# Attention and a gated FFN on one core: batch 1's rounds later in block 0, batch 2's q and k loaded earlier

## The chip, the cores and the metric

The kernel runs on one core of a Trainium2 chip. The metric is the device time of one execution in microseconds. The engines are PE (TensorE, matrix multiply; PEld is its weight load), DVE (VectorE), ACT (ScalarE), POOL (GpSimd) and SP (SyncE, which here only issues DMAs). POOL and ACT issue some DMAs too.

## The reference

```python
# q, k, v: 8 batches, 8 heads, 576 positions, 64 dims, float32
scores = q @ k^T / sqrt(64)            # per batch and head
scores = where(pos_i // 64 >= pos_j // 64, scores, -1e9)
attn = softmax(scores)
x = (attn @ v)                          # heads side by side: [8 * 576, 512]
out = (relu(x @ w_gate) * (x @ w_val)) @ w_out   # 512 -> 1536 -> 512
```

The mask works in blocks of 64 positions: a query sees all keys of its own block and of earlier ones. Inputs and output are float32; the kernel computes in bfloat16 and accumulates in float32.

## The kernel before

**Work units.** A batch has 512 main positions and a tail of 64 (512 to 575). A *round* r handles head pair hp = r % 4 of batch b = r // 4 for the main positions: `visit(r)` computes the transposed scores of both heads on PE, three groups of exp on ACT write `attnT`, `corners(r)` lets DVE clear the masked corners, `head_av(r, hh)` multiplies with v for one head (10 matmuls) and normalises on DVE into `xnat`, and `pe_xT(r)` (four PE transposes and an ACT copy) or `to_xT_dma(r)` (a DMA transpose on SP) puts the result into `xT`, the transposed input of the FFN. `tail_visit`, `tail_av` and `tail_to_xT` do the same for a batch's 64 tail positions, all heads at once.

**The FFN as the clock of the program.** `ffn_gen` (L602) is a generator that yields after each of its matmuls. Block j is the FFN of batch j's main positions: 96 matmuls for gate and value (12 column groups f, for each 4 parts c of gate and 4 of value, where c is the head pair), then 48 for the output (4 row groups s of 12). Block 8 is the FFN of all tails. A *place* p is a count of these matmuls: block j runs from place 144 j to 144 (j + 1). Attention is placed between the matmuls: `run(base, events)` (L758) sorts events by place, issues FFN matmuls up to each place and then calls the event. The rounds of batch b are placed inside block b - 1, so `xT` of batch b must be whole when place 144 b is reached. Only in block 0, f = 0, are the matmuls ordered so that the two of c = 3 come last (L611).

**Order.** All five engines run in the order in which the program is written (`manual_schedule`, L669): an instruction that waits holds up all later ones of its engine. A DMA that waits holds up its issuing engine.

**Loads.** For batches 0 to 3, class `Early` loads float32 into `stage` buffers (ten of them) with DMAs from SP, and an engine casts to bfloat16: `load_qk(h0, n)` and `cast_qk` for n heads from h0 (cast order q, then k), `load_v_packed` and `cast_v_packed` for v of four heads with four positions side by side, which `sort_v` (16 PE matmuls with the selection matrix `sel`, then a DVE and an ACT copy) has to put in order, `load_v` and `cast_v` for v already in order with one DMA for each head, `load_v_chunks` the same for 256 positions of all heads, `load_tails` and `cast_tails`, `cast_v_tail` for the 64 tail positions. q and k are then transposed, by `pe_mains(hp)` on PE (four transposes for q, evacuated by DVE, four for k, evacuated by ACT) or by `transpose` (DMA into `perm`) and `unpermute` (`un`; DVE for q, POOL for k). From batch 4 on, `load_qkv` (L304) loads with casting DMAs from POOL, and `dma_transposes` transposes with DMAs from SP.

**Buffers that matter here.** `psum_ffn` has three banks, shared by gate, value, output, AV and transposes; `ob`, the copy of an output row group that is stored, has three buffers; `q_bf` and `k_bf` have two each; `v_bf`, `qTm`, `kTm`, `qTt`, `kTt` have one for even and one for odd batches. A row group's store is issued when the next row group's copy has been (L645 to L647): that of s = 0 in block 0 at place 120. `put` (L591) issues the stores of batch 0 from POOL, later ones from ACT.

**Block 0 before.** After the first 32 matmuls of the FFN (from L728), the loads of w_out, batch 1's second halves and the tails of batches 0 and 1 are written, then the casts for POOL, in this order: batch 1's q and k of heads 0 to 3, w_gate and w_val's last part, packed v, w_out, batch 1's second q, k and v, all tails. Batch 1's `pe_mains(0)`, `pe_mains(1)` and `sort_v(0)` stand at places 64, 68 and 72, the rounds 4 to 7 at 76, 88, 100 and 118. Batch 2's loads are written at 111 (`load_2`) and its casts at 124 (`mains_2`).

Of the kernel before, what the change touches and what calls it, by code (L numbers as in the profile page):

```python
# [17 lines left out]
def kernel(  # L18
# [10 lines left out]
    nc = tc.nc  # L29
# [89 lines left out]
    class Early:  # L119
# [59 lines left out]
        def cast_qk(self, h0, n, engs):  # L179
            lo = 64 * (h0 % 4)  # L180
            for t in range(2):
                engs[t](  # L182
                    self.half(t, h0 // 4)[:, :, lo : lo + 64 * n].rearrange(
                        "p j (h d) -> p h j d", d=64
                    ),
                    self.st[t, h0].rearrange("p (h j d) -> p h j d", h=n, j=4),
                )
# [414 lines left out]
    def ffn_gen():  # L602
        for j in range(B + 1):
            hT = []
            x = xT_of(j) if j < B else xTt.rearrange("p b h n -> p h b n")
            for f in range(12):
                i, fo = f // 4, 128 * (f % 4)
                gate = psum_ffn.tile([128, 512], FP, name="ffnp")
                val = psum_ffn.tile([128, 512], FP, name="ffnp")
                steps = [(t, c) for t in range(2) for c in range(4)]  # L610
                if j == 0 and f == 0:  # L611

                    steps.sort(key=lambda tc_: tc_[1] == 3)
# [55 lines left out]
    with tc.manual_schedule(engines={E.PE, E.DVE, E.Activation, E.Pool, E.SP}):  # L669
# [60 lines left out]
        e1.load_qk(4, 4)  # L730
        e1.load_v_packed(4)
        for e in (e0, e1):
            e.load_tails((0, 1))
            e.load_tails((2,))
        e1.cast_qk(0, 4, (pool, pool))
        cast_w(w_2, pool)
# [3 lines left out]
        cast_w(w_out[2], pool)  # L740
        e1.cast_qk(4, 4, (pool, pool))
        e1.cast_v_packed(4, pool)
        for e in (e0, e1):
            e.cast_tails((pool, pool))
            e.cast_v_tail(pool)
        ffn(32)
        e1.pe_mains(0, (dve, act))
        ffn(4)
        e1.pe_mains(1, (dve, act))
        ffn(4)  # L750
        e1.sort_v(0, (dve, act))
        ffn(4)
        place = [76]

# [4 lines left out]
        def run(base, events):  # L759
            for p, f in sorted(events, key=lambda e: e[0]):  # L760
                upto(base + p)
                f()

        def round_at(p, r, av, to_xT, late=(), corner_eng=None):

            exps = []

            def begin():
                exps.extend(visit(r))
                exps[0]()  # L770
                exps[1]()

            return [
                (p, begin),
                (p + 6, lambda: exps[2]()),
                (p + 13, lambda: corners(r, corner_eng or nc.vector)),
                (av[0], lambda: head_av(r, 0)),
                (av[1], lambda: head_av(r, 1)),
                (to_xT[0], lambda: to_xT[1](r)),
            ]  # L780
# [23 lines left out]

        early = {}

        def load_2():
            e2 = early[2] = Early(2)
            e2.load_qk(0, 4)
            e2.load_qk(4, 4)  # L810
            e2.load_v_chunks(0)
            e2.load_v_chunks(1)
            e2.load_tails((0, 1))
            e2.load_tails((2,))

        def mains_2():
            e2 = early[2]
            e2.cast_qk(0, 4, (pool, pool))
            e2.cast_qk(4, 4, (pool, pool))
            e2.transpose(0)  # L820
            e2.transpose(1)

        def tails_2():
            e2 = early[2]
            e2.cast_tails((pool, pool))
            e2.transpose_tails()

        def v_2():
            e2 = early[2]
            e2.cast_v_tail(pool)  # L830
            e2.cast_v_chunks(0, pool)
            e2.cast_v_chunks(1, pool)
# [23 lines left out]

        events = []
        for r, p in ((4, 76), (5, 88), (6, 100), (7, 118)):
            end = 20 if r == 6 else 14
            events += round_at(p, r, (p + end + 2, p + end + 6), (p + end + 10, pe_xT))  # L860
        events += [
            (98, lambda: e1.pe_mains(2, (dve, act))),
            (110, lambda: e1.pe_mains(3, (dve, act))),
            (111, load_2),
            (116, lambda: e1.sort_v(4, (dve, act))),
            (124, mains_2),
            (140, lambda: e0.pe_tails((dve, act))),
        ]
        run(0, events)
        events = tail_at(4, 0, (20, 24)) + tail_at(116, 1, (132, 136))  # L870
        for r, p in ((8, 32), (9, 52), (10, 72), (11, 92)):
            events += round_at(p, r, (p + 21, p + 25), (p + 25, to_xT_dma))
        events += [
            (7, lambda: e1.pe_tails((dve, act))),
            (8, tails_2),
# [16 lines left out]
        for b in range(3, B):  # L892
            events = tail_at(120, b, (136, 140))
            if b == 3:
                events += tail_at(50, 2, (69, 73))
            for i, p in enumerate((2, 26, 74, 96) if b == 3 else (2, 32, 62, 92)):
                r = 4 * b + i
                events += round_at(p, r, (p + 20, p + 24), (p + 24, to_xT_dma))
            if b == 3:
                events.append((3, un(3, 2, (dve, pool))))  # L900
                events.append((33, un(3, 3, (dve, pool))))
            if b + 1 < B:
                for at, which in ((4, (0, 1)), (75 if b == 3 else 46, (2,))):
                    events.append((at, lambda b=b, w=which: load_qkv(b + 1, w)))
                events.append((66, lambda b=b: dma_transposes(b + 1)))
            run(144 * (b - 1), events)
# [30 lines left out]
```

## Time and profile before

| | us |
|---|---|
| median of 8 executions | 373.5 (372.23 to 376.93) |
| the profiled execution | 376.93 |
| its span | 375.1 |
| PE busy | 356.6 |
| DVE, ACT, POOL busy | 170.4, 171.3, 119.2 |
| block 0's first matmul (PE) | 20.27 |
| block 1's first matmul | 66.74 |

The profile is one execution, taken by the hardware profiler. A row of a group or of the order of time gives the line of the kernel, the engine, the operation, what is written and read, and how often (x); in the order of time it begins with start and duration in us, and what stands in brackets is the idle time of the engine before it and what ended that. A row of waits names who waited, for whom, the total in us, how many times and the longest. A row of a stretch gives its length and then each engine's busy time. POOL's casts of 128x1024 take 1.04 us each, those of 64x512 0.61; a matmul of 512 columns is issued every 0.216 us at full clock. A DMA row ends with the time from issue to landing.

### The profile page before, as it was taken

To read this page: it belongs to the slowest core of one execution; us is meant where nothing else is said; L and a number is where in the kernel's file an instruction comes from. 1 tells how busy PE (TensorE), PEld (TensorE's weight loads), DVE (VectorE), ACT (ScalarE), POOL (GpSimd) and SP (SyncE) were. 2 spreads that over 40 slices of the span, in tenths; PEclk is the share of its full clock that TensorE was granted. 3 is DMA by queue.
4 is the path that set the end of the run, shared out by engine and by line. 5 is a ranking of instruction groups with operands and counts; after the bars stand their busy time and mean duration, and the time that the engine had idled before them with its cause. 6 is when DMAs were issued, how large, how long until landed. Compare 5 with 4: busy or idle time off the path is not lost.

```text
span 375.1 us, 7513 instructions
## 1 busy us (share of the span) xinstructions
PE 356.6 (95%) x2956; PEld 178.1 (47%) x3004; DVE 170.4 (45%) x392; ACT 171.3 (46%) x283; POOL 119.2 (32%) x156
## 2 busy tenths in 40 slices
PE   7899969999999999699999999999999999999995
PEld 3644434544555545244554445444544454444443
DVE  3644455556555444155334542554345444323432
ACT  5924744576435652355445534653366423302310
POOL 6678776455267174480058003000000000000000
PEclk9999999999999999899999999999999999999999
DMA  8999999979959699999779965845200130020013
GB/s 256 295 371 358 373 202 302 188 177 264 140 130 134 88 130 154 139 125 148 135 95 132 125 128 93 65 78 133 79 16 17 42 100 7 2 84 28 3 34 106
DMA packets 140739, 51.35 MB, mean 137 GB/s; under 512 B 120352, under 2 KB 133920, under 8 KB 140704
## 3 DMA queue, kind: packets, MB, share of 16 engines
q0 software_dynamic: 56576, 8.13, 44.8%
q1 hardware_dynamic: 79424, 34.62, 42.4%
q10 hardware_dynamic: 4704, 8.13, 7.1%
q8 instruction: 23, 0.38, 0.4%
q14 instruction: 12, 0.10, 0.2%
HBM read 37.75 MB, written 9.44 MB: 126 GB/s over the span
## 4 chain that ended last, share of the span: by engine, by line
PE 82%; DMA 10%; POOL 2%; issue 2%; DVE 1%; ACT 1%; SPq 1%; POOLq 0%; DVEq 0%; ACTq 0%
PE ffnp L615 45%; PE ffnp L634 23%; PE ffnp L553 5%; DMA stage<-in_moe_w_val_dram 3%; DMA stage<-in_k_dram 3%; PE sc L426 3%; DMA xT<-xnat 3%; PE ffnp L522 2%; PE one L426 1%; DMA stage<-in_q_dram 1%; PE sc L460 1%; POOL k_bf L182 1%; SPq L132 1%; POOL sel L94 0%; POOL q_bf L182 0%
## 5 line engine op out<-in xcount | busy, mean ns | idle before, releaser
L628 DVE TENSOR_TENSOR hT<-gate_sb,ffnp 128x512 bf16<-128x512 bf16 x108 | 74.2, 687 | 99.6 <-PE ffnp L615 84.3
L624 ACT ACTIVATE gate_sb<-ffnp 128x512 bf16<-128x512 f32 x108 | 65.0, 602 | 105.6 <-PE ffnp L615 105.4
L615 PE MATMUL ffnp<-xT,wg 128*128 128x512 bf16 x369 | 100.7, 382 | 3.9 <-DMA xT<-xnat 3.2
L615 PE MATMUL ffnp<-xT,wv 128*128 128x512 bf16 x376 | 101.6, 382 | 0.7 <-ACT gate_sb L624 0.2
L634 PE MATMUL ffnp<-wo,hT 128*128 128x512 bf16 (+1 forms) x420 | 98.1, 373 | 1.1
L615 PEld LDWEIGHTS <-wv 128*128 128x128 bf16 x432 | 40.3, 98 | 50.2 <-issue 7.3
L615 PEld LDWEIGHTS <-wg 128*128 128x128 bf16 x432 | 40.2, 98 | 47.1 <-issue 4.3
L634 PEld LDWEIGHTS <-hT 128*128 128x128 bf16 x444 | 40.2, 98 | 40.0 <-issue 0.8
L435 ACT ACTIVATE attnT<-sc 128x1024 bf16<-128x1024 f32 x56 | 56.9, 1040 | 0.0
L644 DVE COPY ob<-ffnp 128x512 f32<-128x512 f32 (+1 forms) x37 | 25.1, 677 | 40.8 <-PE ffnp L634 40.4
L316 POOL DMA_DIRECT2D v_bf<-in_v_dram x20 | 16.8, 856 | 64.3 <-PE ffnp L522 48.6
L553 PEld LDWEIGHTS <-attnT 128*128 128x128 bf16 x640 | 26.4, 98 | 15.2 <-DVE xnat L508 4.4
L507 DVE RECIPROCAL recip<-ffnp 128x4 f32<-128x4 f32 (+1 forms) x76 | 13.6, 179 | 37.0 <-PE ffnp L553 26.8
L553 PE MATMUL ffnp<-v_bf,attnT 128*128 128x65 bf16 x600 | 28.2, 194 | 0.4 <-PE sc L460 0.2
L441 ACT ACTIVATE attnT<-one 128x256 bf16<-128x256 f32 x28 | 10.7, 383 | 35.1 <-PE ffnp L426 26.9
L508 DVE TENSOR_TENSOR xnat<-ffnp,recip 128x256 bf16<-128x256 f32 x60 | 25.5, 424 | 2.1
L426 PE MATMUL sc<-qTm,kTm 64*128 64x512 bf16 (+1 forms) x168 | 16.8, 305 | 0.0
L426 PEld LDWEIGHTS <-kTm 64*128 64x128 bf16 x224 | 8.8, 94 | 14.9 <-issue 10.6
L481 ACT ACTIVATE attnTt<-one 64x256 bf16<-64x256 f32 x8 | 3.0, 376 | 28.0 <-PE ffnp L460 28.0
L472 ACT ACTIVATE attnTt<-sc 128x1024 bf16<-128x1024 f32 x16 | 15.6, 1014 | 0.0
L316 POOL DMA_DIRECT2D k_bf<-in_k_dram x16 | 14.1, 897 | 3.9 <-DMA v_bf<-in_v_dram 3.6
L316 POOL DMA_DIRECT2D q_bf<-in_q_dram x16 | 14.3, 918 | 0.1
(88 smaller groups left out, 262.7 us busy)
## 6 DMA issues: line engine op xcount, KB each, us to landing
out_dram<-ob ACTq DMA_DIRECT2D x28, 256.0 KB, 2.3
stage<-in_moe_w_gate_dram SPq DMA_DIRECT2D x6, 512.0 KB, 9.1
stage<-in_moe_w_val_dram SPq DMA_DIRECT2D x6, 512.0 KB, 9.5
stage<-in_q_dram SPq DMA_DIRECT2D x6, 512.0 KB, 6.4
stage<-in_k_dram SPq DMA_DIRECT2D x6, 512.0 KB, 7.3
stage<-in_moe_w_out_dram SPq DMA_DIRECT2D x6, 512.0 KB, 9.6
stage<-in_v_dram SPq DMA_DIRECT2D x8, 256.0 KB, 6.9
q_bf<-in_q_dram POOLq DMA_DIRECT2D x16, 128.0 KB, 6.5
```

The costliest lines, as they stand in the source:

```text
L316: nc.gpsimd.dma_start(dst, src[b, :, 128 * c : 128 * c + n, :].rearrange("h p d -> p h d"),)
L426: nc.tensor.matmul(where[c].rearrange("p (c n) -> p c n", n=128), kTm[b % 2][head_of(hh), c, hp, :], qTm[b % 2][head_of(hh), c:4, hp, :], ...
L435: return lambda: nc.scalar.activation(at[:, :, lo : lo + 512], sc, AF.Exp, scale=scale)
L472: return lambda: nc.scalar.activation(at[:, :, 2 * i : 2 * i + 2, 0:256], main[i].rearrange("p g (h n) -> p g h n", h=2), AF.Exp, scale=scale,
L507: nc.vector.reciprocal(recip, av[:, :, 64])
L508: nc.vector.tensor_tensor(out=out, in0=av[:, :, 0:64], in1=recip.to_broadcast([rows, n, 64]), op=AX.mult,)
L553: nc.tensor.matmul(av[:, p, :], at[:, hh, col : col + 128], vb[:, c, h, :], start=(p == 0), stop=(c == p), skip_group_check=True,)
L615: nc.tensor.matmul((gate, val)[t], (wg, wv)[t][i][:, c, fo : fo + 128], x[:, c], start=(c == 0), stop=(c == 3),)
L624: nc.scalar.activation(gate_sb, gate, AF.Relu)
L628: nc.vector.tensor_tensor(out=h, in0=gate_sb, in1=val, op=AX.mult)
L634: nc.tensor.matmul(op, hT[f][:, 128 * s : 128 * (s + 1)], wo[f // 4][:, f % 4, n0:n1], start=(f == 0), stop=(f == 11),)
L644: nc.vector.tensor_copy(ob, op)
```

## The change

- `cast_qk` may skip q or k; batch 1's k casts move from POOL to DVE, at places 64 (heads 0 to 3) and 115 (heads 4 to 7).
- Batch 1's v heads 4 to 7 are loaded in order (`load_v`, four DMAs) in place of packed; `sort_v(4)` is gone.
- Batch 2's q and k loads come after batch 0's q and k tails and ahead of the other tails; v chunks of batch 2 follow; batch 2's and batch 1's tails come after the first `transpose` of batch 2 on SP. POOL's casts of batch 2's q and k are written before place 32, so they stand ahead of all that POOL issues later, batch 0's stores among it.
- The events of block 0 start at place 32. `pe_mains` of batch 1 move to 70, 74, 118, 122, `sort_v(0)` to 86, the rounds to 90, 106, 125 and 136. Round 6's AVs stand at 142 and 143; its transposes and all of round 7's AVs and transposes at 144. Corners are placed at latest half a place before the first AV. Block 1's first column group has c = 3 last too.
- Batch 1's tail casts move to place 152 and its `pe_tails` from 151 to 244.
- In block 2 the tail of batch 2 moves from place 50 to 3 (counted in the block), rounds 12 and 13 from 2 and 26 to 27 and 50, round 14 from 74 to 73, `un(3, 3)` from 33 to 40, and the v load of batch 4 from 75 to 46.

```diff
@@ -179,6 +179,8 @@
         def cast_qk(self, h0, n, engs):
             lo = 64 * (h0 % 4)
             for t in range(2):
+                if engs[t] is None:
+                    continue
                 engs[t](
                     self.half(t, h0 // 4)[:, :, lo : lo + 64 * n].rearrange(
                         "p j (h d) -> p h j d", d=64
@@ -608,7 +610,7 @@
                 gate = psum_ffn.tile([128, 512], FP, name="ffnp")
                 val = psum_ffn.tile([128, 512], FP, name="ffnp")
                 steps = [(t, c) for t in range(2) for c in range(4)]
-                if j == 0 and f == 0:
+                if j < 2 and f == 0:
 
                     steps.sort(key=lambda tc_: tc_[1] == 3)
                 for t, c in steps:
@@ -728,29 +730,33 @@
         ffn(32)
         w_out = [load_w_out(i) for i in range(3)]
         e1.load_qk(4, 4)
-        e1.load_v_packed(4)
-        for e in (e0, e1):
-            e.load_tails((0, 1))
-            e.load_tails((2,))
-        e1.cast_qk(0, 4, (pool, pool))
+        e1.load_v(4, 4)
+        e2 = Early(2)
+        e0.load_tails((0, 1))
+        e2.load_qk(0, 4)
+        e2.load_qk(4, 4)
+        e0.load_tails((2,))
+        e2.load_v_chunks(0)
+        e2.load_v_chunks(1)
+        e1.cast_qk(0, 4, (pool, None))
         cast_w(w_2, pool)
         e1.cast_v_packed(0, pool)
         cast_w(w_out[0], pool)
         cast_w(w_out[1], pool)
         cast_w(w_out[2], pool)
-        e1.cast_qk(4, 4, (pool, pool))
-        e1.cast_v_packed(4, pool)
-        for e in (e0, e1):
-            e.cast_tails((pool, pool))
-            e.cast_v_tail(pool)
-        ffn(32)
-        e1.pe_mains(0, (dve, act))
-        ffn(4)
-        e1.pe_mains(1, (dve, act))
-        ffn(4)
-        e1.sort_v(0, (dve, act))
-        ffn(4)
-        place = [76]
+        e1.cast_qk(4, 4, (pool, None))
+        e1.cast_v(4, 4, pool)
+        e0.cast_tails((pool, pool))
+        e2.cast_qk(0, 4, (pool, pool))
+        e2.transpose(0)
+        e2.load_tails((0, 1))
+        e2.load_tails((2,))
+        e1.load_tails((0, 1))
+        e1.load_tails((2,))
+        e0.cast_v_tail(pool)
+        e2.cast_qk(4, 4, (pool, pool))
+        e2.transpose(1)
+        place = [32]
 
         def upto(p):
             ffn(p - place[0])
@@ -758,7 +764,7 @@
 
         def run(base, events):
             for p, f in sorted(events, key=lambda e: e[0]):
-                upto(base + p)
+                upto(base + int(p))
                 f()
 
         def round_at(p, r, av, to_xT, late=(), corner_eng=None):
@@ -773,7 +779,7 @@
             return [
                 (p, begin),
                 (p + 6, lambda: exps[2]()),
-                (p + 13, lambda: corners(r, corner_eng or nc.vector)),
+                (min(p + 13, av[0] - 0.5), lambda: corners(r, corner_eng or nc.vector)),
                 (av[0], lambda: head_av(r, 0)),
                 (av[1], lambda: head_av(r, 1)),
                 (to_xT[0], lambda: to_xT[1](r)),
@@ -802,31 +808,15 @@
         def pe_xT(r):
             to_xT_pe(r, (act,))
 
-        early = {}
-
-        def load_2():
-            e2 = early[2] = Early(2)
-            e2.load_qk(0, 4)
-            e2.load_qk(4, 4)
-            e2.load_v_chunks(0)
-            e2.load_v_chunks(1)
-            e2.load_tails((0, 1))
-            e2.load_tails((2,))
-
-        def mains_2():
-            e2 = early[2]
-            e2.cast_qk(0, 4, (pool, pool))
-            e2.cast_qk(4, 4, (pool, pool))
-            e2.transpose(0)
-            e2.transpose(1)
+        early = {2: e2}
 
         def tails_2():
-            e2 = early[2]
             e2.cast_tails((pool, pool))
             e2.transpose_tails()
+            e1.cast_tails((pool, pool))
+            e1.cast_v_tail(pool)
 
         def v_2():
-            e2 = early[2]
             e2.cast_v_tail(pool)
             e2.cast_v_chunks(0, pool)
             e2.cast_v_chunks(1, pool)
@@ -854,24 +844,26 @@
         def un(b, hp, engs=(dve, dve)):
             return lambda: early[b].unpermute(hp, engs)
 
-        events = []
-        for r, p in ((4, 76), (5, 88), (6, 100), (7, 118)):
-            end = 20 if r == 6 else 14
-            events += round_at(p, r, (p + end + 2, p + end + 6), (p + end + 10, pe_xT))
+        events = round_at(90, 4, (110, 114), (118, pe_xT))
+        events += round_at(106, 5, (126, 130), (134, pe_xT))
+        events += round_at(125, 6, (142, 143), (144, pe_xT))
+        events += round_at(136, 7, (144, 144), (144, pe_xT))
         events += [
-            (98, lambda: e1.pe_mains(2, (dve, act))),
-            (110, lambda: e1.pe_mains(3, (dve, act))),
-            (111, load_2),
-            (116, lambda: e1.sort_v(4, (dve, act))),
-            (124, mains_2),
-            (140, lambda: e0.pe_tails((dve, act))),
+            (64, lambda: e1.cast_qk(0, 4, (None, dve))),
+            (70, lambda: e1.pe_mains(0, (dve, act))),
+            (74, lambda: e1.pe_mains(1, (dve, act))),
+            (86, lambda: e1.sort_v(0, (dve, act))),
+            (115, lambda: e1.cast_qk(4, 4, (None, dve))),
+            (118, lambda: e1.pe_mains(2, (dve, act))),
+            (122, lambda: e1.pe_mains(3, (dve, act))),
+            (143.5, lambda: e0.pe_tails((dve, act))),
         ]
         run(0, events)
         events = tail_at(4, 0, (20, 24)) + tail_at(116, 1, (132, 136))
         for r, p in ((8, 32), (9, 52), (10, 72), (11, 92)):
             events += round_at(p, r, (p + 21, p + 25), (p + 25, to_xT_dma))
         events += [
-            (7, lambda: e1.pe_tails((dve, act))),
+            (100, lambda: e1.pe_tails((dve, act))),
             (8, tails_2),
             (16, un(2, 0, (dve, pool))),
             (44, un(2, 1, (dve, pool))),
@@ -892,15 +884,15 @@
         for b in range(3, B):
             events = tail_at(120, b, (136, 140))
             if b == 3:
-                events += tail_at(50, 2, (69, 73))
-            for i, p in enumerate((2, 26, 74, 96) if b == 3 else (2, 32, 62, 92)):
+                events += tail_at(3, 2, (21, 25))
+            for i, p in enumerate((27, 50, 73, 96) if b == 3 else (2, 32, 62, 92)):
                 r = 4 * b + i
                 events += round_at(p, r, (p + 20, p + 24), (p + 24, to_xT_dma))
             if b == 3:
-                events.append((3, un(3, 2, (dve, pool))))
-                events.append((33, un(3, 3, (dve, pool))))
+                events.append((2, un(3, 2, (dve, pool))))
+                events.append((40, un(3, 3, (dve, pool))))
             if b + 1 < B:
-                for at, which in ((4, (0, 1)), (75 if b == 3 else 46, (2,))):
+                for at, which in ((4, (0, 1)), (46, (2,))):
                     events.append((at, lambda b=b, w=which: load_qkv(b + 1, w)))
                 events.append((66, lambda b=b: dma_transposes(b + 1)))
             run(144 * (b - 1), events)
```

## The prediction

> **What bounds the kernel now.** I read the page first, then the stretches of 10 us, then who TensorE (PE) waited for, then the order of time on POOL and DVE around 56 to 67 us and on PE around 150 us.
>
> ```profile
> PE 356.6 (95%) x2956; PEld 178.1 (47%) x3004; DVE 170.4 (45%) x392; ACT 171.3 (46%) x283; POOL 119.2 (32%) x156
> PEclk9999999999999999899999999999999999999999
> ```
> PE is busy for 95% of the span, so the end moves only with what makes PE wait, with its clock, or with its number of matmuls. The 8 in the clock row is the one place where the granted clock was not full.
>
> ```profile
> 30.00:40.00 10.00, 8.32 (x62) 4.12 (x62) 4.55 (x7) 3.89 (x7) 8.77 (x12) 1.00 1.08 368
> 40.00:50.00 10.00, 7.56 (x65) 3.52 (x65) 4.68 (x13) 6.58 (x12) 7.30 (x7) 1.00 1.14 312
> ...
> 150.00:160.00 10.00, 6.77 (x35) 2.81 (x32) 1.73 (x5) 4.15 (x7) 4.96 (x6) 0.83 2.62 138
> ```
> The first number after the length is PE's busy time, the number before the last two the clock. PE idles 1.7 and 2.4 us in the first two rows (another 0.6 between 50 and 66 us, 4.7 in all between 27 and 66.7), and 3.2 us at 150, where the clock falls too.
>
> ```profile
> PE ffnp L615 <- DMA xT<-xnat: 3.2, 1, 3.2
> PE ffnp L281 <- POOL k_bf L182: 2.1, 2, 1.5
> ...
> PE ffnp L281 <- POOL q_bf L182: 1.0, 1, 1.0
> ...
> PE sc L229 <- POOL v_p L209: 0.8, 1, 0.8
> ```
> So the waits are batch 1's casts (L281 and L229, in block 0) and one DMA transpose (L615, at the start of block 3).
>
> ```profile
> 150.14 0.39 PE L615 MATMUL ffnp<-xT,wg 128*128 128x512 bf16 x1
> 153.76 0.44 PE L615 MATMUL ffnp<-xT,wg 128*128 128x512 bf16 x1 [3.23 <-DMA xT<-xnat]
> 153.99 1.91 PE L615 MATMUL ffnp<-xT,wv 128*128 128x512 bf16 x4
> ```
> After that wait 4 matmuls take 1.91 us; at full clock they take 1.03. The clock stood at one half for 3.4 us (153.94 to 157.35), which costs 1.7. Wait and clock: 4.9 us.
>
> **Own time and median.** The profiled execution took 376.93 us, its span 375.1, so 1.8 lie around the span. It is the slowest of the eight shown (372.23 to 376.93, median 373.5). That spread, 4.7, is as large as the 4.9 just found, and the wait is a race between a transpose and loads; I take it that the faster executions have little of it. Without it the profiled one would have taken 372.0, which I use as floor.
>
> **The change, part by part.**
>
> *Block 0, place 32 to 96.* PE reaches place 32 at 27.2 us and place 64 at 34.1, as before. The k cast of heads 0 to 3 goes to DVE. DVE cast 128x512 in 0.43 us (its one L182 row), so 1024 takes about 0.8; it starts at 35.1, after the product of f=7, and PE has the q transposes of place 70 done at 35.6. PE waits 0.4 if DVE runs freely. DVE copies from SBUF beside POOL (L266) took 0.59 in the median and 1.66 at worst, so up to 1.1 more; I take 0.5 more, ends 0.4 and 1.5. The second k cast (emitted at 115) costs PE another 0.3 by the same rows, ends 0 and 1.3.
> The row came first: DVE's SBUF copies beside POOL sometimes take 1.07 longer. The Trainium skill, "SBUF — State Buffer", section "Who interferes with whom", says that a DVE cast in a two-port mode and any GpSimd instruction exclude each other for a whole instruction. By that rule each of the two casts would wait for a POOL cast (1.04 at most), 2.1 us in the worst case, where my sum has 1.2; the rule speaks against moving casts to DVE while POOL casts without a gap.
>
> *w_out.* Six casts end on POOL at 46.5 us, paced by landings 1.35 apart. PE now gets to place 104 at about 45.9 (fifth cast ends 45.1) and, after round 5's scores, to f=10 at 47.1: no wait, ends 0 and 0.5.
>
> *sort_v(4) goes*: 16 matmuls, 0.55 us of PE, one DVE and one ACT copy off the path. The unsorted load is 4 DMAs on SP of 128 KB; eight such landed 0.57 apart at the start (9.8 to 13.8), so 2.3 us where the packed load took 2.5 (48.8 to 51.3): nothing, hidden by 5 us before round 6 needs it at place 142.
>
> *Order of c in block 1.* Six matmuls, 1.3 us, now stand before the first that reads head pair 3; they cover the ACT copy of 0.59. That is a gain of up to 0.6 for the chain below.
>
> *End of block 0.* Rounds 6 and 7 end at place 144. From round 7's scores (time T) PE has 5.3 us of work: scores 0.7, eight matmuls 1.7, four AV groups at 0.5, two times four transposes 0.5, tail transposes 0.3. But corners(7) must await two exps of ACT (0.8 + 1.04 + 1.04, until T+2.9), AV 7 follows at T+4.7, both normalisations (0.62 each) stand on DVE behind the copy of ob (0.69), and PE transposes xnat at T+6.7: 1.6 us of wait, ends 0.5 and 2.5. Adding the 0.55 of sort_v, the old waits (4.7) and the new ones (0.9 + 0.3 + 1.6, and 0.7 of PSUM turns), block 1 would start 1.7 us earlier than its 66.74, at 65.0.
>
> *The store, which stands in the way.* Batch 0's stores are issued by POOL, in program order.
>
> ```profile
> 56.10 0.72 POOL L594 DMA_DIRECT2D out_dram<-ob  x1
> 56.81 1.05 POOL L182 CAST q_bf<-stage 128x1024 bf16<-128x1024 f32 x1
> ...
> 61.44 1.04 POOL L182 CAST k_bf<-stage 128x1024 bf16<-128x1024 f32 x1 [0.59 <-DMA stage<-in_k_dram]
> 62.43 0.55 POOL L594 DMA_DIRECT2D out_dram<-ob  x1
> ```
> ```profile
> 66.94 0.69 DVE L644 COPY ob<-ffnp 128x512 f32<-128x512 f32 x1 [0.90 <-PE ffnp L634]
> ```
> ```profile
> out_dram<-ob POOLq DMA_DIRECT2D x1, 256.0 KB, 6.3
> ...
> out_dram<-ob POOLq DMA_DIRECT2D x1, 256.0 KB, 4.5
> ...
> out_dram<-ob POOLq DMA_DIRECT2D x1, 256.0 KB, 4.7
> ...
> out_dram<-ob POOLq DMA_DIRECT2D x1, 256.0 KB, 5.6
> ```
> The four answers are the four stores, issue to landing. ob has three buffers, so the fourth copy (s=3, at 66.94) may start only when the first store has landed: 56.10 + 6.3 = 62.4, 4.5 us to spare. In the new order all four casts of batch 2's q and k, and batch 0's v tail ahead of the last two, stand on POOL before that first store. When do they end? Batch 1's last k lands at 48.8 as before (its cast starts at 48.83); unsorted v 2.3; two tails at 0.7 (six took 4.2, 51.3 to 55.5); batch 2's four loads 5.9 (55.5 to 61.4): 58.4; the v tail 0.7: 59.1. Then casts of 0.61, 1.04, 1.04 end at 61.8. The store lands 4.5 to 6.3 later, 66.3 to 68.1, with the mean (5.3) 67.1. DVE reaches the fourth ob copy at about 62.5 and is held there; behind it queue both normalisations of round 7, for which PE waits. Block 1 starts after 0.69 + 0.62 + 0.62 + 0.3 of semaphores and transposes: at 69.3, 2.6 us later than 66.74, ends 1.0 and 4.0. PE stands for about 5 us, longer than the 3.2 that cost the clock at 150, so again 1.7 (nearest row; ends 0 and 3.4, once or twice the half-speed stretch).
> The skill's "TensorE: Matmul & The Clock Gate", section "What's actually happening", puts the limit at an idle window of about 3.4 us and says that the window runs freely; the row above lost the clock after 3.2. By that rule a stand of 5 us nearly always costs the clock, by the row alone often.
>
> *SP and POOL besides.* Four transposes of batch 2's perm now stand on SP ahead of the tails of batches 2 and 1, and wait for POOL until 61.8; behind them are only loads and transposes that PE needs from place 160 on, at 73 us or later: nothing. Batch 1's three tail casts (0.61 each) move to place 152 on POOL, PE needs them at 244: nothing.
>
> *Batch 3.* The tail of batch 2 moves from place 50 to 3, rounds 12 and 13 to 27 and 50; the same PE work. v_bf of batch 4 becomes free at place 313 instead of 361, so POOL issues v(4), then q(5) and k(5), from about 119 us instead of 129.5.
>
> ```profile
> k_bf<-in_k_dram POOLq DMA_DIRECT2D x1, 128.0 KB, 15.9
> xT<-xnat SPq DMA_TRANSPOSE x1, 10.3
> ```
> The last xT transpose of batch 3 (issued 143.44) took 10.3 us among these loads, and PE can wait 7 without loss. Ten us earlier, most of them have landed by then; other xT transposes beside loads took 6.0 to 7.6 (issued at 115.9, 161.9, 200.6). So the wait at 150 goes, ends 0 and all 4.9 kept.
>
> **Sum.** 376.93 - 4.9 (wait at 150) + 2.6 (block 1 starts later) + 1.7 (clock) = 376.3. Against the median, where I count most of the 4.9 as absent, 372.0 + 4.3 = 376.3: 0.7% slower than 373.5. About 0.5% (1.9 us) is what a measurement of this kernel can tell from no change.
>
> **Rivals.**
> 1. *The store comes in time* (the faster side). Place: the fourth ob copy. It decides from a landing before 64.3 (64.3 + 2.3 = 66.6, the old start); for this batch 2's last k and the v tail must land 2 to 3 us earlier, at 56.5. Against: 4.1 MB (seven loads of 512 KB, three of 128) from 45.4 on would need 366 GB/s, where the stretches 40 to 50 and 50 to 60 us show 312 and 259. Time: 372.0 - 1.7 = 370.3.
> 2. *The spread is not the wait at 150*, that is, the median execution has it too. Then the change takes 4.9 off the median and adds 4.3: 372.9, no change.
> 3. *The wait at 150 stays*, because the b=4 transposes and the earlier loads slow each other: 15 loads took 31 us beside transposes (129.5 to 160.7), so from 119 they could last to 150. Time: 376.3 + 4.9 = 381.2; with half of it 378.8.
>
> **How the numbers follow.** Forecast 0.52 (374.2 to 378.5 by the ends of its terms; one part in eight of it below 375.4), rival 1 0.15, rival 2 0.16, rival 3 0.17. Faster by over 0.5% (under 371.6): rival 1 and a little of rival 2, 0.18. Within 0.5% (to 375.4): most of rival 2 and an eighth of the forecast, 0.2. Slower: 0.62. The range 370.0 to 380.0 leaves out the upper part of rival 3 and the fringe below rival 1.
>
> **What would show it.** Right: in block 0 the fourth ob copy on DVE starts just after a landing of out_dram<-ob, about 67 us, with POOL's first L594 near 62; PE's longest wait is at L573 for xnat; the half clock moves from 154 to about 69; PE has no wait for xT<-xnat at 150. Wrong: the first store is issued before 59, or ob is not waited for; or L615 still waits for xT at block 3.

## The result, and the profile after

The changed kernel takes 378.96 us (median of 11 executions, 377.79 to 383.27). The kernel before takes 374.4 in the same comparison (32 executions, 371.57 to 378.43). The ratio is 1.014, with a 95% interval of 1.011 to 1.017: slower. The profiled execution of the changed kernel took 379.41, its span is 377.3.

The head of the page, and the row of the granted clock:

```profile
PE 357.4 (95%) x2940; PEld 179.2 (48%) x2988; DVE 172.8 (46%) x393; ACT 171.4 (45%) x282; POOL 116.4 (31%) x154
PEclk9999999599999999999999999999999999999999
```

PE has 16 matmul records fewer (`sort_v(4)`) and yet 0.8 us more of busy time: part of its work ran slowly. The clock row tells where. The low digit has moved from the start of block 3 to the seam of blocks 0 and 1, and it is lower. The stretches of 10 us (length, then busy time of PE, PEld, DVE, ACT and POOL, granted clock, DMA share, GB/s):

```profile
30.00:40.00 10.00, 9.68 (x56) 4.81 (x56) 5.34 (x9) 4.06 (x7) 8.36 (x11) 1.00 1.08 367
40.00:50.00 10.00, 9.95 (x86) 4.56 (x86) 4.20 (x11) 6.66 (x11) 6.25 (x6) 1.00 1.02 300
...
60.00:70.00 10.00, 3.24 (x59) 2.73 (x58) 3.53 (x12) 1.65 (x3) 4.34 (x6) 0.77 1.29 233
70.00:80.00 10.00, 9.67 (x106) 5.13 (x106) 2.97 (x6) 4.85 (x8) 5.05 (x7) 0.71 0.88 120
...
150.00:160.00 10.00, 9.37 (x82) 4.79 (x82) 3.50 (x8) 4.30 (x7) 4.46 (x6) 1.00 1.59 180
```

The first two rows are what the change does well: PE idles 0.4 us there, where it idled 4.1. In the third it stands for 6.8 of 10 us. In the fourth it is busy, at a clock of 0.71. The stretch at 150 is mended. The waits of PE name the place:

```profile
PE ffnp L555 <- DVE ob L646: 4.9, 1, 4.9
...
PE ffnp L575 <- DVE xnat L510: 0.9, 2, 0.7
...
PE ffnp L617 <- DMA xT<-xnat: 0.6, 1, 0.6
```

And the order of time on POOL and on DVE shows what the copy of `ob` itself waited for:

```profile
60.10 0.61 POOL L219 CAST v_bf<-stage 64x512 bf16<-64x512 f32 x1 [3.25 <-DMA stage<-in_v_dram]
60.66 1.04 POOL L184 CAST q_bf<-stage 128x1024 bf16<-128x1024 f32 x1
61.64 1.04 POOL L184 CAST k_bf<-stage 128x1024 bf16<-128x1024 f32 x1
62.63 1.81 POOL L596 DMA_DIRECT2D out_dram<-ob  x3
```
```profile
67.38 0.69 DVE L646 COPY ob<-ffnp 128x512 f32<-128x512 f32 x1 [5.09 <-DMA out_dram<-ob]
```

POOL stands 3.25 us for the load of batch 0's v tail, casts it and the last two casts of batch 2, and only then issues three stores in a row, at 62.63. The first lands 4.7 later. Until then DVE cannot copy the fourth row group out of its PSUM bank, and the second AV of round 7 waits for that bank. On PE, at the seam:

```profile
62.74 0.46 PE L555 MATMUL ffnp<-v_bf,attnT 128*128 128x65 bf16 x10 [0.63 <-ACT kTt L304]
68.12 0.71 PE L555 MATMUL ffnp<-v_bf,attnT 128*128 128x65 bf16 x10 [4.92 <-DVE ob L646]
...
69.57 0.61 PE L575 MATMUL ffnp<-ident,xnat 128*128 128x128 bf16 x4 [0.74 <-DVE xnat L510]
69.97 1.49 PE L617 MATMUL ffnp<-xT,wg 128*128 128x512 bf16 x3
```

The same ten matmuls take 0.46 us before the wait and 0.71 after it. Block 1 starts at 69.97 in place of 66.74. The clock stood at one half from 65.5 to 75.7 us, three times the 3.4 us that it stood at half in the execution before.

The table gives each block's first matmul, in the profiled executions, with the two that a later section needs.

| first matmul of block, us | before | after | store_first | tails_late |
|---|---|---|---|---|
| 0 | 20.27 | 20.50 | 20.57 | 21.30 |
| 1 | 66.74 | 69.97 | 64.75 | 65.79 |
| 2 | 108.01 | 114.79 | 111.27 | 107.20 |
| 3 | 148.96 | 155.82 | 152.30 | 148.23 |
| 4 | 192.67 | 195.23 | 191.91 | 187.06 |
| profiled execution | 376.93 | 379.41 | 376.09 | 371.23 |

### The profile page after: what moved, and what is told of

It is laid out like the page before. It is cut to its first block, busy times and chain, and to the rows that moved or that the text cites. A ratio compares the mean times of both kernels' runs of the same rounds, so it can differ in the third digit from the quotient of the medians.

```text
span 377.3 us, 7479 instructions
## 1 busy us (share of the span) xinstructions
PE 357.4 (95%) x2940; PEld 179.2 (48%) x2988; DVE 172.8 (46%) x393; ACT 171.4 (45%) x282; POOL 116.4 (31%) x154
## 3 DMA queue, kind: packets, MB, share of 16 engines
q1 hardware_dynamic: 81008, 34.62, 43.5%
## 4 chain that ended last, share of the span: by engine, by line
PE 78%; DMA 14%; POOL 3%; SPq 2%; issue 2%; ACT 1%; DVE 1%; POOLq 0%; DVEq 0%; ACTq 0%
PE ffnp L617 45%; PE ffnp L636 20%; PE ffnp L555 4%; DMA stage<-in_v_dram 3%; DMA stage<-in_moe_w_val_dram 3%; PE sc L428 3%; DMA xT<-xnat 2%; DMA stage<-in_moe_w_out_dram 2%; PE ffnp L524 2%; DMA stage<-in_q_dram 1%; PE one L428 1%; DMA out_dram<-ob 1%; SPq L155 1%; PE sc L462 1%; SPq L132 1%
## 5 line engine op out<-in xcount | busy, mean ns | idle before, releaser
L555 PEld LDWEIGHTS <-attnT 128*128 128x128 bf16 x640 | 26.6, 98 | 19.9 <-issue 6.4
L555 PE MATMUL ffnp<-v_bf,attnT 128*128 128x65 bf16 x600 | 28.4, 194 | 6.0 <-DVE ob L646 4.9
```

The lines of the kernel that those rows point to most:

```text
L555: nc.tensor.matmul(av[:, p, :], at[:, hh, col : col + 128], vb[:, c, h, :], start=(p == 0), stop=(c == p), skip_group_check=True,)
```

## The experiments

Every run is compared with the kernel before on the same chip. Medians are given with the ratio to it.

**store_first: the first store ahead of the late casts.** This undoes the one piece of order that the prediction blames: batch 0's v tail and the second casts of batch 2 are written behind place 120, where the first store is issued.

```diff
         e1.load_tails((2,))
-        e0.cast_v_tail(pool)
-        e2.cast_qk(4, 4, (pool, pool))
-        e2.transpose(1)
...
+        def rest_2():
+            e0.cast_v_tail(pool)
+            e2.cast_qk(4, 4, (pool, pool))
+            e2.transpose(1)
...
+            (120, rest_2),
```

> The changed kernel, with the cast of batch 0's v tail, the casts of batch 2's q and k of heads 4 to 7 and their DMA transposes written at place 120, so that they stand on POOL behind the first store and not ahead of it; the stores stay on POOL. Theory (POOL's order is what delays the store): the first store is issued at about 57 and lands near 62, block 1 starts near 64.7, no half clock, 370 to 372. Rival 1 (stores from POOL are slow beside the loads, whatever stands ahead of them): it lands after 65 and block 1 starts after 67. Rival 2 (the chain of round 7 is too long by itself): over 377.

Measured: 373.55 us, ratio 0.998 (0.996 to 1.002). That is 5.4 less than the changed kernel. POOL, then DVE:

```profile
57.08 0.71 POOL L596 DMA_DIRECT2D out_dram<-ob  x1
...
75.70 0.61 POOL L219 CAST v_bf<-stage 64x512 bf16<-64x512 f32 x1 [1.29 <-DMA stage<-in_v_dram]
76.26 2.03 POOL L268 COPY kTm<-perm 128x512 bf16<-128x512 bf16 x2
```
```profile
62.23 0.68 DVE L646 COPY ob<-ffnp 128x512 f32<-128x512 f32 x1
```

The copy has no bracket now: DVE did not stand before it. Block 1 starts at 64.75 and the clock is full there. So the store wait, with its clock, is shown as the cause of the loss. It isn't all. The profiled execution (376.09, the longest of the ten) has a new wait, before the scores of round 8:

```profile
77.35 0.28 PE L428 MATMUL one<-qTm,kTm 64*128 64x256 bf16 x1 [3.53 <-POOL kTm L268]
```

It ends with POOL's copy of `kTm`, which stands in POOL's queue behind batch 1's tail casts. The last of these waited for its load until 75.7, while the transposed k had landed at 69.27. Half a clock for 3.4 us follows. In the changed kernel PE reaches round 8 only at 81.67, where it would be at 73.8 here without the wait, and finds `kTm` ready.

**busy: PE kept at work during the wait.** 22 matmuls of 512 columns, whose result nobody reads, stand between the two AVs of round 7.

```diff
+    def busy(n):
+        jp = psum_sc.tile([128, 2, 512], FP, name="sc")
+        for _ in range(n):
+            nc.tensor.matmul(jp[:, 0], ident, wo[0][:, 0], start=True, stop=True)
...
-        events += round_at(136, 7, (144, 144), (144, pe_xT))
+        events += round_at(136, 7, (144, 144.2), (144.6, pe_xT))
+        events += [(144.1, lambda: busy(22))]
```

> The changed kernel with 22 matmuls of 512 columns, whose result nobody reads, between the two AV groups of round 7, where PE stood for 4.9 us. They fill the wait and don't shorten it. Theory (the wait costs twice, by itself and by the half clock after it, of which 5.7 us lay on busy PE): block 1 starts at the same 69.9, no half clock, and the time falls by 2.9 to about 376.1. Rival (the half clock costs little, since PE catches up in waits of block 1): under 1 us. If the 22 matmuls last longer than the wait, block 1 starts later by what is over.

Measured: 376.74 us, ratio 1.007 (1.004 to 1.010), 2.2 less than the changed kernel. The stretches at the seam:

```profile
60.00:70.00 10.00, 8.11 (x83) 4.82 (x84) 3.53 (x12) 2.21 (x5) 4.33 (x6) 1.00 1.29 234
70.00:80.00 10.00, 8.72 (x110) 4.74 (x113) 5.48 (x8) 4.95 (x9) 8.02 (x11) 1.00 0.86 116
```

The clock is 1.00 in both. Block 1 starts at 69.54, so the wait for the store is still there (DVE stood 4.62 us before the same copy), and only the clock's part has gone. The two costs of the stand are thus separate, and the clock's is 2.2 us by the medians, 2.6 by the start of block 2 in the two profiled executions (114.79 and 112.16).

**store_act: the stores of batch 0 from ACT's queue.**

```diff
-            (nc.gpsimd if j == 0 else nc.scalar).dma_start(out[r0 : r0 + 128, :], ob)
+            nc.scalar.dma_start(out[r0 : r0 + 128, :], ob)
```

> The changed kernel, with batch 0's stores issued by ACT instead of POOL. Theory (the fourth copy of ob is held by the first store, which stands on POOL behind batch 2's casts): the copy, at 67.4 us in the changed kernel, comes at about 62.3, block 1 starts near 64.7 instead of 69.9, the half clock (10.2 us of it, 5.7 with PE busy) goes, and the time is 379.0 - 5.2 - 2.9 = 370.9, with up to 0.8 more from block 1; about 1% under the kernel before. Rival (the chain of round 7 at the end of block 0 is too long by itself, the store only ends at the same moment): block 1 still starts after 68 and the time stays over 377.

Measured: 385.65 us, ratio 1.031 (1.026 to 1.036). The expectation missed by 15 us, on the wrong side. The order of time on ACT:

```profile
52.66 0.59 ACT L286 COPY kTm<-ffnp 128x512 bf16<-128x512 bf16 x1 [0.54 <-PE ffnp L283]
...
65.70 0.37 ACTq L596 DMA_DIRECT2D out_dram<-ob  x1
66.11 0.59 ACT L286 COPY kTm<-ffnp 128x512 bf16<-128x512 bf16 x1 [12.87 <-DMA perm<-q_bf]
```

ACT stood for 12.87 us and issued its first store the moment that a DMA transpose of batch 2 had landed, with which the store has no data in common. In the trace the DMAs of SP and ACT signal their landing on eight counters, which they take in turn. The store's turn comes eight after that transpose's, so it has the same counter, and ACT waits for this counter first. A DMA that waits holds its engine, so all of ACT's copies and exps waited with it, and PE for them (10.8 us at L555, for `kTm`). Block 1 starts at 78.10. So the store was not saved by taking it from POOL; it got a worse queue.

**act_sp_late: is it the order in the program that gives the store that counter?** Batch 2's `transpose` calls and the tail loads are written behind the store, at place 144.

```diff
-        e2.transpose(0)
-        e2.load_tails((0, 1))
...
+        def rest_sp():
+            e2.transpose(0)
+            e2.load_tails((0, 1))
...
+            (144, rest_sp),
```

> Batch 0's stores on ACT as in the first variant, but all that SP had ahead of them from batch 2's first transpose on (four transposes and the tail loads of batches 2 and 1) is written at place 144, behind the stores; tail casts late as in the late-tails variant. In the first variant ACT stood 12.9 us, until batch 2's first transpose had landed at 65.6, before it issued its first store, and PE 10.8 us behind it. Theory (a DMA issued by ACT or SP takes one of eight landing counters in the order in which the program is written, and waits until the DMA that had it last has landed; so a store from ACT waits for one of the loads that SP has in flight): ACT now waits only for the load eight DMAs before it, batch 2's k of heads 0 to 3, landing near 56; PE stands about 3 us near place 121, and the time is 372 + 3 = 375. Rival (ACT's DMAs are slow beside SP's as such): ACT is held past 60 us again and the time is over 380.

Measured: 386.65 us, ratio 1.035 (1.028 to 1.042), as slow as store_act. ACT's waits:

```profile
ACT kTm L286 <- DMA perm<-q_bf: 14.1, 1, 14.1
```

Again the store went out when `perm<-q_bf` had landed. So the idea that a DMA of another queue written later can't hold the store is refuted. The turns in the trace are those of store_act: the store comes eight behind the transpose, although it is written ahead of it. That an ACT store waits for the SP transpose that has its counter is shown twice; what sets the order of the turns, since the order of writing doesn't, stays open.

**before_order: the casts alone, on the kernel before.** Only batch 2's q and k loads, casts and transposes are written ahead of place 64; rounds, DVE casts and the unsorted v are left as before.

```diff
             e.cast_v_tail(pool)
+        e2 = Early(2)
+        e2.load_qk(0, 4)
+        e2.load_qk(4, 4)
+        e2.cast_qk(0, 4, (pool, pool))
+        e2.cast_qk(4, 4, (pool, pool))
+        e2.transpose(0)
+        e2.transpose(1)
```

> The kernel before with one part of the change alone: batch 2's q and k loads, casts and DMA transposes written before place 64, so that all four casts stand on POOL ahead of the first store of batch 0; rounds and the rest as before. Theory (the store costs because block 0 ends earlier in the changed kernel and not by the order alone): the first store is issued at about 62.5 and lands near 67; the fourth copy of ob, wanted at 66.9, waits 0 to 1.5 us, and since before's rounds end ahead of place 144, block 1's first matmuls don't wait for it at all: under 1.0 us over before (374.4), no half clock. Rival (the order alone costs the 5 us): 378 or more.

Measured: 377.95 us, ratio 1.011 (1.006 to 1.017). The theory was right for block 0 and missed what comes behind it. The first store landed at 68.08 and the fourth copy of `ob` started at 68.18 (the profile puts its idle time down to PE, but PE was done before); block 1 nevertheless started at 67.13, because round 7's normalisations were done before that copy. (In this execution block 0 had started only at 23.62, behind 6.8 us at half clock; it then took 43.5 us where before took 46.5.) Then:

```profile
77.73 0.61 POOL L192 CAST q_bt<-stage 64x512 bf16<-64x512 f32 x1 [12.73 <-DMA stage<-in_q_dram]
78.28 0.61 POOL L192 CAST k_bt<-stage 64x512 bf16<-64x512 f32 x1
78.84 2.05 POOL L266 COPY kTm<-perm 128x512 bf16<-128x512 bf16 x2
```
```profile
PE one L426 <- POOL kTm L266: 3.2, 1, 3.2
```

POOL waited 12.73 us for batch 2's tail load, which SP issues behind its waiting transposes, and the copy of `kTm`, ready long before, waited with it. PE's 3.2 us and half a clock for 3.4 us make 4.9, as much as lies between the two medians on this chip (373.03 for before). It is the wait of store_first again, in another kernel: the early casts bring it with them.

**tails_late: store_first, and the tail casts behind the copies of `kTm`.**

```diff
             e2.transpose_tails()
+
+        def tails_1():
             e1.cast_tails((pool, pool))
...
-            (8, tails_2),
+            (17, tails_2),
+            (45, tails_1),
```

> The previous variant (first store ahead of batch 2's last casts on POOL), in which batch 2's tail casts are written at place 161, after the first unpermute of batch 2, and batch 1's tail casts at place 189, after the second. In the previous variant block 1 started at 64.7 as expected, but PE then stood 3.5 us at the scores of round 8 for kTm, whose POOL copy (76.3 us) queued behind batch 1's tail casts, and the clock fell to one half for 3.4 us. Theory (the order on POOL is the whole of that wait; the transposed k had landed at 69.3): the wait and the half clock go, 373.6 - 3.5 - 1.7 = 368.3. Rival (the transposes of batch 2 on SP are what comes late): PE still waits over 1.5 us before round 8 and the time is over 371.

Measured: 371.99 us, ratio 0.994 (0.991 to 0.997), 1.6 less than store_first. POOL:

```profile
69.80 1.07 POOL L268 COPY kTm<-perm 128x512 bf16<-128x512 bf16 x1 [4.94 <-DMA perm<-k_bf]
```

The copy now starts with the landing, 6.5 us earlier than in store_first; the wait before round 8 and the half clock behind it are gone. The expectation of 368.3 was set too low by its base: it took the 5.2 us of store_first's profiled execution, the longest of that kernel, from store_first's median. From that execution's own 376.09 it would have been 370.9, and the profiled execution of tails_late took 371.23.

**before_block2: the last part alone, on the kernel before** (the tail of batch 2 at place 3 of block 2, rounds 12 and 13 at 27 and 50, `un(3, 3)` at 40, the v load of batch 4 at 46).

```diff
-                events += tail_at(50, 2, (69, 73))
+                events += tail_at(3, 2, (21, 25))
```

> The kernel before with only the change of block 2 (tail of batch 2 at 3, rounds 12 to 14 at 27, 50, 73, the v load of batch 4 at 46). Theory (the casting loads of batches 4 and 5 collide with the last xT transpose of batch 3; the median of before, 374.4, holds about half of the 4.9 us that the profiled execution lost there, the fastest none): the wait at block 3 falls under 1 us, no half clock there, and the time is 371.5 to 372.6, with less spread than before's 371.6 to 378.4. Rival 1 (before's spread is not this wait): 374.4 - 4.3 = 370.1 or the same spread. Rival 2 (earlier loads collide as well): 374 or more.

Measured: 372.61 us, ratio 0.996 (0.993 to 0.998). PE has no wait for `xT` at block 3 any more. The part is worth 1.8 us by the medians, not 4.9. The profiled execution (373.08) has a half clock all the same, for 3.4 us from 49.9, in block 0, which this edit doesn't touch:

```profile
48.28 0.40 PE L281 MATMUL ffnp<-ident,q_bf 128*128 128x128 bf16 x4 [0.94 <-POOL q_bf L182]
50.12 0.61 PE L281 MATMUL ffnp<-ident,k_bf 128*128 128x128 bf16 x4 [1.45 <-POOL k_bf L182]
```

The same two waits of before, 0.95 and 1.49 us, were followed by no half clock.

**before_again: the kernel before, unchanged, profiled a second time.**

> The kernel before, unchanged, for a second profile. Theory (its spread of 371.6 to 378.4 is above all the wait at the start of block 3, 0 to 3.2 us and a half clock of up to 1.7): this execution's time less its wait for xT there and less half of the half clock after it is 372.0 within 1 us. Rival: wait and half clock there are as in the first profile (4.9) although the time is near the median, or are absent although the time is over 374.

Measured: 372.64 us in that execution. In the window from 100 to 170 us, PE's wait at the start of block 3, and the stretch in which the clock had been 0.83:

```profile
PE ffnp L615 <- DMA xT<-xnat: 0.2, 1, 0.2
```
```profile
150.00:160.00 10.00, 9.73 (x71) 4.49 (x70) 4.42 (x11) 6.30 (x12) 8.48 (x11) 1.00 3.01 139
```

The same transpose took 7.3 us here where it had taken 10.3. So the 4.9 is a race that some executions lose, as the prediction assumed. Less its wait the execution took 372.4, within the 1 us expected. But the race isn't all of the spread: in this execution block 0 started 2.1 us later than in the first, with a half clock of its own before it, and in before_block2, without the race, the times still run from 370.93 to 374.74.

**packed: tails_late with v heads 4 to 7 packed and `sort_v(4)` at place 135.**

```diff
-        e1.load_v(4, 4)
+        e1.load_v_packed(4)
...
+            (135, lambda: e1.sort_v(4, (dve, act))),
```

> The same as the late-tails variant, but v heads 4 to 7 of batch 1 loaded packed again and put in order by the 16 matmuls, at place 135. Theory (sort_v costs its PE time and no more, the load is hidden either way): 0.55 us more than the late-tails variant, 368.9. Rival (its two copies on DVE and ACT delay round 7 at the end of block 0): 1.5 us more or over.

Measured: 371.94 us, ratio 0.994 (0.992 to 0.996), against 371.99 for tails_late. The 0.55 us of 16 matmuls is not resolved: inconclusive in size, and at most small. (The 368.9 went by the 368.3 that tails_late was expected to take.)

**earlier: tails_late with batch 1's rounds 2 to 7 places earlier.**

```diff
-        events += round_at(125, 6, (142, 143), (144, pe_xT))
-        events += round_at(136, 7, (144, 144), (144, pe_xT))
+        events += round_at(119, 6, (133, 135), (138, pe_xT))
+        events += round_at(129, 7, (141, 142), (144, pe_xT))
```

(Rounds 4 and 5 go to 88 and 102, the DVE cast and `pe_mains` 4 to 5 places earlier.)

> The same with the rounds of block 0 placed 2 to 7 places earlier (88, 102, 119, 129; the AVs of round 7 at 141 and 142). Theory (the end of block 0 holds 1.6 to 2 us of waits because rounds 6 and 7 end at its last place): block 1 starts 1 to 2 us before 64.7, with no new wait at the w_out casts (last at 46.6) or for k of heads 4 to 7 (landed 48.6): 366.5 to 367.5. Rival (the later places are needed by the loads): waits at the casts return and the time is 368.3 or more.

> The variant with the earlier rounds, first store ahead of batch 2's last casts and tail casts after the unpermutes, again, for a closer interval: 370.5 to 371.5, 0.6 to 1.0% under the kernel before. If the 0.9 us under the late-tails variant were chance, it comes out at 372.

Measured: 371.04 us, ratio 0.992 (0.989 to 0.996), and in the second set 371.19, ratio 0.994 (0.992 to 0.997). It beats both kernels, the changed one by 2%. Against tails_late the gain of 0.8 to 1 us lies within the intervals, and by the ratios the second set has none (0.994 for both), so no gain over tails_late is shown. The expected 1 to 2 us at the start of block 1 didn't come: it starts at 64.86, as in store_first. PE's waits between 50 and 70 us suggest why:

```profile
PE ffnp L555 <- DVE attnT L497: 1.4, 2, 0.8
PE ffnp L283 <- ACT xT L580: 0.5, 1, 0.5
PE ffnp L575 <- DVE xnat L510: 0.3, 1, 0.3
```

In tails_late the wait for `xnat` was 1.1. It is 0.3 now, and 1.4 for the cleared corners has taken its place: it seems that the chain from scores to exp, corners, AV and normalisation is as long as before, and only the point where PE waits for it has moved.

## Why the prediction was right, and where its sizes were off

The forecast was 376.3, slower by 0.7%; it is 378.96, slower by 1.4%, inside the range. The side and the mechanism are right, and store_first shows it.

The working was against a profiled execution without the wait at block 3, 372.0. By the block starts of the two profiled executions the sum is: 372.0 + 3.2 (block 1 starts later, of which 0.2 lies ahead of block 0) + 3.6 (block 1 takes 44.82 us for 41.27: 2.7 by the clock, 0.8 otherwise) + 0.6 (wait at block 3) = 379.4, the profiled execution's 379.41. By the medians the change costs over 6 us against before_block2 (372.61), where the prediction's sum has 4.3 against its floor of 372.0. Term by term:

- *The store's time*: POOL issue at 61.8 predicted, 62.63 measured; landing 67.1 predicted, 67.29 measured. The v tail's load came 1 us later than the estimate from the loads' pace. The landing fits by luck in part: the issue was 0.8 later, and the store 0.6 quicker (4.66 us) than the mean that the prediction took.
- *The end of block 0 without the store*: 65.0 predicted; 64.75 in store_first. The waits for casts that the change removes are gone as predicted: between 20 and 60 us PE's largest is 0.5.
- *Block 1's start, 2.6 later predicted, 3.2 measured.* The start is at 69.97 where 69.3 was predicted. The step left out that the copy frees a PSUM bank: I had PE wait for `xnat` at the transposes, but it waits a step earlier, with the second AV of round 7, which needs that bank. From the copy's start to block 1 it is 2.6 us, not 2.2; the AV and the transposes ran at half clock.
- *The clock, 1.7 predicted, 2.7 measured in block 1, with some 0.5 more in the 3.2 above.* The stand of 5 us kept the clock at half not for 3.4 us, the nearest row, but for 10.2. In this time PE was at work for 6.6 us, 1.1 ahead of block 1 and 5.45 in it. (The 5.7 that the expectations of store_act and busy call busy is how long block 1 ran at half clock.) That is the term that failed most; its upper end, 3.4, held it. By busy, 2.2 of it is in the median. Why the clock came back only at 75.7 isn't shown; PE still stood for 0.74 and 0.33 us between 68.1 and 73.4. "Nearly always" was too much for the rule that the prediction named: a window of 3.4 us that runs freely lies whole in a stand of 4.9 in under half of the cases (1.5 of 3.4, an estimate). The runs show that less than a whole idle window is enough: 3.2 us in before, 0.94 and 1.45 in before_block2.
- *Block 1 beyond the start and the clock, 0 predicted, 0.8 measured.* A cost without a term: the late tail and q, k casts of POOL now run back to back beside the copies of batch 2's q. One of these copies, and what POOL did during most of it:

```profile
90.00 2.84 DVE L268 COPY qTm<-perm 128x512 bf16<-128x512 bf16 x1
```
```profile
90.35 1.06 POOL L268 COPY kTm<-perm 128x512 bf16<-128x512 bf16 x1
91.36 1.04 POOL L184 CAST q_bf<-stage 128x1024 bf16<-128x1024 f32 x1
```

  The three other copies of batch 2's q, beside which POOL stood idle, took 0.6 us each. PE waited 0.35 for the long one and 0.3 for what stood behind it on DVE.
- *The two k casts on DVE*: 0.9 us of PE's time (0.4, and 0.5 for POOL beside them) and 0.3 predicted. They took 0.84 and 0.68 us, and PE's waits between 20 and 60 us name neither: overestimated for this execution. POOL was casting during only 0.4 and 0.3 us of them, so they say little of the exclusion that the prediction weighed with the Trainium skill, "SBUF — State Buffer", "Who interferes with whom". The other traces agree with it: the nine that have these casts show them at 0.68 to 1.36 us (PE waited up to 0.7 for one, in tails_late), and of the 104 copies of q from `perm` on DVE in all thirteen traces the 49 beside which POOL stood idle took 0.59 to 0.61 us, the 55 others 0.59 to 2.91. No run was made to test it alone.
- *The wait at block 3, 4.9 gone predicted*: 0.6 left, and the clock full. The transposes there are not much faster for it: the last three of batch 3 took 8.9, 9.4 and 7.7 us, where the last two took 11.2 and 10.3 before. The right size for medians is another matter. before_block2 gives 1.8, so about two thirds of the 4.9 that I took off the profiled execution isn't in the median. The forecast counted most of it as absent, which held; rival 2, that the median has all of it, fell.
- *Rival 1, the store in time* (370.3), fell for the change as written. Its time isn't reached by the store's place alone: store_first gave 373.55, since POOL's queue held the next wait, and only with the tail casts moved too it is 371.99 (tails_late).
- *Tail casts of batch 1 on POOL at place 152, costed at nothing*: PE's need of them at 244 was looked at, not what stands behind them on POOL. With the store wait gone they cost 1.6 us by the medians (store_first to tails_late).

What is left unsettled: tails_late is 0.6 us under before_block2, where the prediction had 1.7 for the rounds' new places and `sort_v`. The two medians come from different chips, and the difference is no larger than their intervals, so whether the new places gain anything by themselves wasn't shown.

## What to carry to other kernels

When work is written earlier on an engine that also issues DMAs, follow what then stands behind it: here four casts ahead of a store, three output buffers and one PSUM bank turned a gain of 2 us (block 1 at 64.75 in place of 66.74) into a stand of 5 us. Removing the wait shows the next one in the same queue, so read the order of time on that engine again after every repair, and give a queue's work in the order in which its inputs land and its results are needed. A store on another engine's queue is not free either: here it waited for the DMA of SP that last had its landing counter, and held all that its engine computes.

## What the runs showed of the hardware that was not expected

- A wait of 3.2 to 3.5 us cost half a clock for 3.4 us (before, store_first, before_order), a stand of 5 us one for 10.2 us; the half clocks beside the stands of 10.8 and 12.1 us (store_act, act_sp_late) lasted 10.2 and 13.7. All are multiples of 3.41. Shorter waits can cost it too: 0.94 and 1.45 us, 0.4 us of work apart, cost 3.4 us in before_block2, and nearly the same two cost nothing in before. 22 unread matmuls in the stand kept the clock full.
- A store issued by ACT waited 12.9 and 14.1 us for a DMA transpose issued by SP with other data, in two kernels. In both traces the DMAs of the two engines took eight landing counters in turn, and POOL's took eight others.
- A DMA transpose of one `xT` took 10.3 us in one execution of the kernel before and 7.3 in another, beside loads of the same program.
- A DVE copy between SBUF buffers took 2.84 us beside POOL's copies and casts, where it takes 0.59 to 0.61 whenever POOL stands idle (49 copies in thirteen traces); 32 of the 55 copies beside a working POOL took over 0.7 us, up to 2.91.
